# Band attention and two gated layers on one core: another order of the first loads

## The chip, the cores and the metric

The kernel runs on one core of one Trainium2 chip, as one program. The metric is the device time of one execution in microseconds (us): the median of several runs. A core has five engines with instruction streams of their own: TensorE (PE in the profile, its weight loads PEld), VectorE (DVE), ScalarE (ACT), GpSimd (POOL) and SyncE (SP, which here only issues loads). They meet through semaphores. Loads issued by SP go, in the order of issue, through one queue that all 16 DMA engines of the core serve.

## The reference, cut to what matters

There are 2 batches, 8 heads, 768 positions and 64 values for each head. Attention looks at a band of 16 positions to either side, and at one summary of each block of 32 positions: the maximum of the keys and the mean of the values.

```
k_sum = k.reshape(B, H, nb, block, D).max(axis=3)
v_sum = v.reshape(B, H, nb, block, D).mean(axis=3)
scores = [banded q @ k.T * scale ,  q @ k_sum.T * scale + log(block)]
x = softmax(scores) @ [v ; v_sum]                    # 1536 tokens x 512
x = (sigmoid(x @ w_gate) * (x @ w_val)) @ w_out      # 512 -> 1536 -> 512
y = max(x @ w1, x @ w2, x @ w3) @ w_out2             # 512 -> 768 -> 512
```

## The kernel before

**Units.** Attention is cut into 16 units (b, p, a): a batch, a pair of heads, a half of the 768 positions. Units 0 to 3 are batch 0, first half, pairs 0 to 3; units 4 to 7 its second half; units 8 to 15 are batch 1. A unit needs its keys (`kn`: all keys of a pair, for batch 1 also `kw`, windows laid out for it), its queries (`q`) and its value windows (`v`); a pair needs its values once more as whole rows (`vn`), for the block means. PE multiplies keys and queries (`scores`; the part `ks` against block maxima that DVE takes from `kn`), DVE takes maxima (L597), ACT exponentials (L603), DVE or ACT divides, PE transposes (L622), ACT copies (`at`), PE multiplies with the values (`pv`, L632), and ACT and DVE write the result as a high and a low part into a tile `x`. For batch 0 the block means come from PE: `vsum`, eight matmuls of `vn` with the constant `avg` (L520); for batch 1 POOL adds up rows first (L525).

**Weights.** A load `raw` brings 128x1024 words; DVE packs it in three operations (L405, L410, L414) into `c`; ACT (L348) and DVE (L351) split it into a high and a low part `w`. There are three buffers `raw`, two `c`, twelve `w`.

**Layers.** A projection of layer 1 (L711) is twelve matmuls of 128x384, into one of four PSUM banks `m`; it needs `x` of all four pairs of a half. Eight projections of a half (four gates, four values) make four tiles `h`; then `B` (L745) multiplies these with the weights of the output. First half, then second half, then the next group of four.

**Who sets the order.** Nothing is scheduled by hand and nothing while the program runs: `Plan.order` simulates the engines when the kernel is built, with a duration and a due time for each task, and writes the tasks down in that order. Each engine then works strictly in it. Constants such as `KEYS0` or `WLOAD0` say by how much a load is due ahead of its unit or weight. Where PE would wait for a tile in the first 45 us of the plan, the plan lets it run matmuls on zeros (`idle`, L994), whose result is overwritten.

Of the kernel before, what the change touches and what calls it, by code (L numbers as in the profile page):

```python
# [9 lines left out]
F32 = mybir.dt.float32  # L10
# [8 lines left out]
WIN = 16  # L19
# [8 lines left out]
LAST = 2  # L28
LASTACC = 12
KEYS0, KEYS = 14.0, 24.0  # L30
SUMS0, SUMS = 14.0, 8.0
ROWS0, ROWS = 2.0, 4.0
WLOAD = 24.0
WLOAD0 = 2.0
WREADY = 8.0
FREE_M = 2
BY_ACT = 6
# [3 lines left out]
SLACK = {"PE": 0.05, "DVE": 0.12, "ACT": 0.1, "POOL": 0.0, "SP": 0.0}  # L41
OVER = 0.0
BANKS_H, BANKS_W, BANKS_T = 7, 12, 5
BANKS_KW, BANKS_KN, BANKS_Q, BANKS_V = 2, 4, 3, 3


class Buf:
# [25 lines left out]
class Plan:  # L73
# [3 lines left out]
    LAT = {"PE": 0.0, "DVE": 0.13, "ACT": 0.05, "POOL": 0.1}  # L77
    CROSS = 0.17
    DMA = 0.95
    TABLE = 1.3  # L80

    def __init__(self):
# [2 lines left out]
    def add(self, eng, dur, due, fn, deps=(), new=(), uses=(), after=(), tab=None):  # L85
        t = Task(eng, dur, due, fn, [d for d in deps if d], list(new), list(uses), [d for d in after if d], tab)
        self.tasks.append(t)
        return t
# [26 lines left out]
    def order(self):  # L115
        engs = ("PE", "DVE", "ACT", "POOL", "SP")
        free = dict.fromkeys(engs, 0.0)
        free["SP"] = 0.6
        dge = ring = 0.0
        clock = self.Clock()  # L120
        free["PE"] = 1.13
        tab = "E"
        taken = {}
        wait, then, ready = {}, {}, {e: [] for e in engs}
        for t in self.tasks:
            pre = t.deps + t.after
            wait[t] = len(pre)
            for d in pre:
                then.setdefault(d, []).append(t)
            if not pre:  # L130
                ready[t.eng].append(t)
        out = []

        def earliest(t):
            at = free[t.eng]
            for d in t.deps:
                at = max(at, d.end + self.lag(d, t))
            for d in t.after:
                at = max(at, d.start)
            need = {}  # L140
            for b in t.new:
                k = need.get(b.tag, 0)
                need[b.tag] = k + 1
                used = taken.setdefault(b.tag, [])
                i = len(used) + k - b.n
                if i >= 0:
                    for d in used[i].users:
                        if d.end is None:
                            return None
                        at = max(at, d.end + (0.1 if d.eng != t.eng else 0.0))  # L150
            return at

        def pressing(x):
            return x[1].due + (SWITCH if x[1].tab and x[1].tab != tab else 0.0)

        while len(out) < len(self.tasks):
            best = None
            for e in engs:
                c = [(at, t) for at, t in ((earliest(t), t) for t in ready[e]) if at is not None]
                if not c:  # L160
                    continue
                first = min(at for at, _ in c)
                at, t = min((x for x in c if x[0] <= first + SLACK[e]), key=pressing)
                if best is None or at < best[0]:
                    best = at, t
            at, t = best
            ready[t.eng].remove(t)
            t.start = at
            t.end = at + t.dur
            if t.eng == "PE":  # L170
                if t.new and at < 45.0:
                    width = min(384, t.new[0].shape[-1] * (t.new[0].shape[1] if len(t.new[0].shape) == 3 else 1))
                    now = free["PE"]
                    while True:
                        end = clock.run(now, width / 2400.0, 1.0, False)
                        if end > at + OVER:
                            break
                        now = clock.run(now, width / 2400.0, 1.0) + 0.001
                        t.idle += 1
                    at = t.start = max(at, now)  # L180
                t.end = clock.run(at, t.dur, t.rows)
            if t.dma:
                dge = max(dge, at) + t.dma
                ring = max(ring, dge + 0.65) + (t.dur if t.eng == "SP" else 0.2)
                free[t.eng] = at + t.dur if t.eng != "SP" else dge + 0.025
                t.end = ring
            if t.tab and t.tab != tab:
                tab = t.tab
                t.end += self.TABLE
            if not t.dma:  # L190
                free[t.eng] = t.end
            for b in t.new:
                taken[b.tag].append(b)
            out.append(t)
            for d in then.get(t, ()):
                wait[d] -= 1
                if not wait[d]:
                    ready[d.eng].append(d)
        return out
# [3 lines left out]
def kernel(  # L203
# [15 lines left out]
    nc = tc.nc  # L219
    B, NPAIR, _, S = qt.shape  # L220
    D = vw.shape[-1]
# [6 lines left out]
    GF = 4  # L228
    NG = NF1 // GF
    TPU = HALF // 128  # L230
# [156 lines left out]
    def convert():  # L387
# [3 lines left out]
        def to_float(ck, t):  # L391
# [23 lines left out]
                    out=c.t, in0=half(r, 0), scalar=29, in1=c.t, op0=ALU.logical_shift_right, op1=ALU.bitwise_or)  # L415

            n += 1
            l = add("SP", 1.456, t - WLOAD - WLOAD0 * (n <= 10), load, new=[r], after=[prev.get("l")])
            k1 = add("DVE", 0.335, t - 2.7, c1, [l], [c], [r], [prev.get("1")])
            k2 = add("DVE", 0.602, t - 2.3, c2, [k1], [], [c, r])  # L420
            k3 = add("DVE", 0.602, t - 1.6, c3, [k2], [], [c, r])
# [69 lines left out]
        chain[tag] = t  # L491
        return t

    def load_task(tag, n, shape, src, dur, t):
        b = Buf(ap_, shape, F32, tag, n)

        def fn(what=tag):
            nc.sync.dma_start(out=b.t[0:src.shape[0]], in_=src)

        return b, after(tag, add("SP", dur, t, fn, new=[b]))  # L500

    kblock, vblock, pvs = {}, {}, {}
    attention = []

    def make_sums(b, p, T):

        kt, lk = load_task("kn", BANKS_KN, [128, S + 2 * WIN], kn[b, p], 1.14, T - (KEYS if b else KEYS0))
        r, lr = load_task("vn", 2, [96, 2, 8 * D], vn[b, p], 1.092, T - (SUMS if b else SUMS0))
        ks = Buf(ap_, [128, NB], F32, "ks", 4)
        vs = Buf(ap_, [128, 2 * D], F32, "vs", 4)  # L510
        ps = psum_s([128, 2 * D])
# [24 lines left out]
        if b == 0:  # L536
            v1, v2 = None, add("PE", 1.75, T - 5, vsum, [lr, built], [ps], [r])
        else:
            lr.after.append(pvs[4 + p])
            vr = Buf(ap_, [96, 2, D], F32, "vr", 2)  # L540
            v1 = add("POOL", 2.5, T - 8, vadd, [lr, built], [vr], [r])
            v2 = add("PE", 0.22, T - 5, vmean, [v1], [ps], [vr])
# [5 lines left out]
    def make_unit(u, i):  # L548
# [3 lines left out]
            make_sums(b, p, T)  # L552
        whole = b == 0
        ks, kk, kt, lk = kblock[b, p]
        if not whole:
            kt, lk = load_task("kw", BANKS_KW, [128, TPU, 2, CW], kw[b, p, a], 1.024, T - KEYS)
        q, lq = load_task("q", BANKS_Q, [128, HALF], qt[b, p, :, HALF * a:HALF * a + HALF], 0.546,
                          T - (KEYS0 if whole else KEYS))
        vt, lv = load_task("v", BANKS_V, [CW, TPU, 2, 2, D], vw[b, p, a], 0.82, T - (ROWS0 if whole else ROWS))
        vs, kv = vblock[b, p]  # L560
        e = [Buf(ap_, [128, TPU, CW], F32, f"e{h}", 2) for h in range(2)]
        nm = Buf(ap_, [128, 2, TPU], F32, "nm", 2)
# [392 lines left out]
        add("ACT", 0.52, due[key] + 4.5, store, [l], [o], [ps])  # L955

    built = add("POOL", 5.0, -100.0, build_consts)
    for i, u in enumerate(units):
        make_unit(u, i)
    convert()  # L960
# [94 lines left out]
```

## Time and profile before

| | us |
|---|---|
| median of 3 runs (564.14, 566.11, 566.13) | 566.11 |
| the profiled execution | 564.06 |
| its span, first to last instruction | 562.3 |
| PE busy | 543.9 (97% of the span) |
| DVE busy | 430.7 (77%) |
| ACT busy | 286.8 (51%) |
| POOL busy | 16.1 (3%) |

The shares are means over stretches with different limits: PE waits mostly in the first 80 us. A matmul's end is modelled, so a busy PE can hide short waits.

### The profile page before, as it was taken

What the parts mean: (1) busy time and instruction counts of PE and PEld (TensorE: products, weight loads), DVE (VectorE), ACT (ScalarE), POOL (GpSimd) and SP (SyncE); (2) the same over time, 40 slices, a digit from 0 to 9 for tenths busy, and PEclk for the clock granted to TensorE, in tenths of its full rate; (3) what the DMA queues carried; (4) which work ended last, traced back from release to release, by engine and by line L of the source; (5) the groups of instructions that cost most, each with busy time, mean ns of one, the idle gap of its engine ahead of it and who ended that gap; (6) DMA issues with size and microseconds to landing.
All of it is one profiled execution on the core that took longest, in us unless ns stands there. A gap on an engine that the chain in (4) does not pass through costs nothing.

```text
span 562.3 us, 10192 instructions
## 1 busy us (share of the span) xinstructions
PE 543.9 (97%) x3924; PEld 521.4 (93%) x3924; DVE 430.7 (77%) x987; ACT 286.8 (51%) x663; POOL 16.1 (3%) x30
## 2 busy tenths in 40 slices
PE   8689899999999999999999999999999999999997
PEld 7578799999999999999999999999999999997886
DVE  6789958894697598949996996799999997885000
ACT  4689776583765656966441332435344333453111
POOL 2001221100000000000000000000000000000000
PEclk9999999999999999999999999999999999999999
DMA  8999653563266453520652553120322222000111
GB/s 296 318 268 283 201 174 135 166 208 113 81 195 187 141 150 110 170 75 1 188 186 78 155 182 114 53 98 21 108 87 87 77 74 82 32 1 37 57 72 60
DMA packets 24288, 71.96 MB, mean 128 GB/s; under 512 B 2736, under 2 KB 6192, under 8 KB 24240
## 3 DMA queue, kind: packets, MB, share of 16 engines
q1 hardware_dynamic: 21120, 67.58, 38.7%
q10 hardware_dynamic: 3120, 3.74, 1.9%
q8 instruction: 31, 0.51, 0.4%
q14 instruction: 17, 0.14, 0.1%
HBM read 67.57 MB, written 3.15 MB: 126 GB/s over the span
## 4 chain that ended last, share of the span: by engine, by line
PE 81%; DVE 7%; DMA 5%; ACT 5%; issue 1%; SPq 1%; ACTq 0%; DVEq 0%
PE m L711 30%; PE m L745 16%; PE s L835 11%; PE m L835 11%; PE m L942 9%; DMA vn<-in_vn_dram 3%; PE s L632 2%; DMA raw<-in_wts_dram 1%; DVE c L414 1%; DVE c L410 1%; PE s L622 1%; ACT e L617 1%; ACT e L603 1%; DVE c L405 1%; PE s L590 1%
## 5 line engine op out<-in xcount | busy, mean ns | idle before, releaser
L711 PE MATMUL m<-x,w 128*128 128x384 f32 x1152 | 211.0, 338 | 0.5 <-ACT t L725 0.3
L711 PEld LDWEIGHTS m<-x,w 128*128 128x128 f32 x1152 | 198.7, 188 | 2.5 <-issue 0.6
L745 PE MATMUL m<-h,w 128*128 128x384 f32 x576 | 107.3, 338 | 0.7 <-DVE h L351 0.7
L745 PEld LDWEIGHTS m<-h,w 128*128 128x128 f32 x576 | 99.3, 188 | 2.0 <-DVE h L351 1.4
L348 ACT ACTIVATE w<-c 128x512 fp32r<-128x512 f32 x96 | 58.1, 610 | 71.6 <-DVE c L414 48.4
L351 DVE TENSOR_TENSOR w<-c,w 128x512 fp32r<-128x512 f32 x96 | 63.8, 665 | 12.6 <-ACT w L348 12.4
L414 DVE SCALAR_TENSOR_TENSOR c<-raw,c 128x512 int32<-128x512 int32 x96 | 66.7, 697 | 0.6
L410 DVE SCALAR_TENSOR_TENSOR c<-raw,c 128x512 int32<-128x512 int32 x96 | 66.0, 689 | 0.6
L835 PE MATMUL m<-x,w 128*128 128x384 f32 x294 | 56.3, 335 | 1.2 <-ACT t L850 1.2
L835 PE MATMUL s<-f,w 128*128 128x384 f32 x294 | 56.0, 334 | 0.0
L835 PEld LDWEIGHTS m<-x,w 128*128 128x128 f32 x294 | 51.3, 188 | 1.6 <-ACT t L850 1.5
L835 PEld LDWEIGHTS s<-f,w 128*128 128x128 f32 x294 | 51.4, 188 | 0.0
L405 DVE TENSOR_SCALAR c<-raw 128x512 int32<-128x512 int32 x96 | 41.7, 437 | 5.7 <-DMA raw<-in_wts_dram 4.7
L725 ACT ACTIVATE t<-m 128x384 f32<-128x384 f32 x48 | 23.4, 491 | 35.2 <-PE m L711 34.8
L730 DVE TENSOR_TENSOR t<-m,t 128x384 f32<-128x384 f32 x48 | 26.6, 554 | 15.3 <-PE m L711 10.8
L348 ACT ACTIVATE h<-t 128x384 fp32r<-128x384 f32 x48 | 24.9, 521 | 25.7 <-DVE t L730 23.8
L603 ACT ACTIVATE e<-e,nm 128x120 f32<-128x120 f32 x96 | 36.6, 384 | 1.3 <-DVE nm L597 1.1
L351 DVE TENSOR_TENSOR h<-t,h 128x384 fp32r<-128x384 f32 x48 | 26.9, 563 | 5.4 <-ACT h L348 5.4
L952 ACT ACTIVATE c<-m 128x512 f32<-128x512 f32 (+1 forms) x13 | 7.3, 565 | 40.0 <-PE m L942 39.6
L850 ACT ACTIVATE t<-s 128x384 f32<-128x384 f32 x27 | 13.3, 491 | 24.4 <-PE s L835 24.4
L942 PE MATMUL m<-w,x 128*128 128x512 f32 (+1 forms) x126 | 24.9, 359 | 0.0
L942 PE MATMUL m<-w,f 128*128 128x512 f32 x108 | 24.7, 389 | 0.0
(108 smaller groups left out, 586.4 us busy)
## 6 DMA issues: line engine op xcount, KB each, us to landing
raw<-in_wts_dram SPq DMA_DIRECT2D x96, 512.0 KB, 4.3
v<-in_vw_dram SPq DMA_DIRECT2D x16, 288.0 KB, 4.8
kn<-in_kn_dram SPq DMA_DIRECT2D x8, 400.0 KB
vn<-in_vn_dram SPq DMA_DIRECT2D x8, 384.0 KB
q<-in_qt_dram SPq DMA_DIRECT2D x16, 192.0 KB, 5.2
kw<-in_kw_dram SPq DMA_DIRECT2D x8, 360.0 KB, 10.0
out_dram<-c ACTq DMA_DIRECT2D x11, 256.0 KB, 2.0
v<-vs ACTq DMA_DIRECT2D x8, 72.0 KB
```

The source lines that it names most:

```text
L348: nc.scalar.activation(out=dst, in_=src, func=ACTF.Copy)
L351: nc.vector.tensor_tensor(out=dst, in0=src, in1=h.bitcast(F32), op=ALU.subtract)
L405: nc.vector.tensor_scalar(out=c.t, in0=half(r, 1), scalar1=5, scalar2=2, op0=ALU.logical_shift_left, op1=ALU.logical_shift_right)
L410: nc.vector.scalar_tensor_tensor(out=c.t, in0=half(r, 1), scalar=-0x40000000, in1=c.t, op0=ALU.bitwise_and, op1=ALU.bitwise_or)
L414: nc.vector.scalar_tensor_tensor(out=c.t, in0=half(r, 0), scalar=29, in1=c.t, op0=ALU.logical_shift_right, op1=ALU.bitwise_or)
L603: nc.scalar.activation(out=e[h].t[:, t], in_=e[h].t[:, t], func=ACTF.Exp, scale=-1.0, bias=nm.t[:, h, t:t + 1], accum_out=sm.t[:, h, t:t + 1])
L711: nc.tensor.matmul(ps.t, lhsT=w.t.rearrange("p s (k f) -> p s k f", k=KC)[:, wh, kc], rhs=src[kc // 2].t[:, xh, kc % 2], start=(kc == 0 an ...
L725: k1 = after("t", add("ACT", 0.371, end, lambda: nc.scalar.activation(out=s.t, in_=ps.t, func=ACTF.Sigmoid), [l], [s], [ps], tab="S"))
L730: k2 = after("t", add("DVE", 0.469, end, lambda: nc.vector.tensor_tensor(out=t.t, in0=ps2.t, in1=s.t, op=ALU.mult), [l2, k1], [t], [ps2, s]))
L745: nc.tensor.matmul(ps.t, lhsT=w.t.rearrange("p s (k f) -> p s k f", k=KC)[:, wh, dm], rhs=h.t[:, xh], start=(i == 0 and j == 0), stop=(i = ...
L835: nc.tensor.matmul(ps.t, lhsT=w.t[:, wh, c:c + 128], rhs=x.t[:, xh, kc], start=new and n == 0, stop=n == 5, skip_group_check=True)
L942: nc.tensor.matmul(ps.t[:, c0:c1], lhsT=h.t[:, xh, e, c:c + 128], rhs=w.t[:, wh, c0:c1], start=(f == 0 and i == 0), stop=(f == NF2 - 1 and ...
```

## The change

**Rows for the means.** The `vn` of batch 0 no longer have two buffers of their own: their loads go into the ring of eight tiles `x`, and take its first four places (they are issued as `x<-in_vn_dram`). Batch 1 keeps one buffer `vn`.

**First weights.** The first four weight loads are due one us behind the keys of units 0 to 3, not as early as possible; the rest of the first twelve by `WLOAD0`, now 12.

**Batch 1 held back.** The loads of unit i of batch 1 may stand in the order only behind the start of `pv` of unit i - 4, and `kn` and `vn` of a pair behind `pv` of unit 4 + p; before, only `vn` was held.

**The plan.** Due times of `vn` and `v` of batch 0 move (`SUMS0`, `ROWS0`), `v` has four buffers, and the plan takes transfers for 1.2 times as long. Since the plan decides the order, all engines' orders change. On PE the idle matmuls, 48 of 128 columns, 27 of 128 and 3 of 384 before, become 11 of 360, all ahead of the first scores.

```
-SUMS0, SUMS = 14.0, 8.0
-ROWS0, ROWS = 2.0, 4.0
+SUMS0, SUMS = 12.0, 8.0
+ROWS0, ROWS = 10.0, 4.0
-WLOAD0 = 2.0
+WLOAD0 = 12.0
-BANKS_KW, BANKS_KN, BANKS_Q, BANKS_V = 2, 4, 3, 3
+BANKS_KW, BANKS_KN, BANKS_Q, BANKS_V = 2, 4, 3, 4
...
+    SLOW = 1.2
...
-                ring = max(ring, dge + 0.65) + (t.dur if t.eng == "SP" else 0.2)
+                ring = max(ring, dge + 0.65) + (t.dur * self.SLOW if t.eng == "SP" else 0.2)
...
-            l = add("SP", 1.456, t - WLOAD - WLOAD0 * (n <= 10), load, new=[r], after=[prev.get("l")])
+            at = target[units[n - 1]] - KEYS0 + 1.0 if n <= NPAIR else t - WLOAD0 if n <= 3 * GF else t - WLOAD
+            l = add("SP", 1.456, at, load, new=[r], after=[prev.get("l")])
...
+    def make_rows(p):
+        r = Buf(xp, [96, 2, 8 * D], F32, "x", 8)
+        vrows[p] = r, after("x", add(
+            "SP", 1.092, target[0, p, 0] - SUMS0, lambda: nc.sync.dma_start(out=r.t, in_=vn[0, p]), new=[r]))
...
-        kt, lk = load_task("kn", BANKS_KN, [128, S + 2 * WIN], kn[b, p], 1.14, T - (KEYS if b else KEYS0))
-        r, lr = load_task("vn", 2, [96, 2, 8 * D], vn[b, p], 1.092, T - (SUMS if b else SUMS0))
+        kt, lk = load_task("kn", BANKS_KN, [128, S + 2 * WIN], kn[b, p], 1.14, T - (KEYS if b else KEYS0), [pvs[NPAIR + p]] if b else [])
+        if b == 0:
+            r, lr = vrows[p]
+        else:
+            r, lr = load_task("vn", 1, [96, 2, 8 * D], vn[b, p], 1.092, T - SUMS, [pvs[NPAIR + p]])
...
+        held = [] if whole else [pvs[i - NPAIR]]
         if not whole:
-            kt, lk = load_task("kw", BANKS_KW, [128, TPU, 2, CW], kw[b, p, a], 1.024, T - KEYS)
+            kt, lk = load_task("kw", BANKS_KW, [128, TPU, 2, CW], kw[b, p, a], 1.024, T - KEYS, held)
...
+    for p in range(NPAIR):
+        make_rows(p)
```

On SP, at the very start of the program, the first twelve loads before (the numbers tell tiles apart; `raw` is a weight, the rest belongs to batch 0):

```order
L398 DMA raw_119<-in_wts_dram 128x1024
L498 DMA kn_121<-in_kn_dram 128x800
L498 DMA vn_123<-in_vn_dram 96x1024
L498 DMA q_125<-in_qt_dram 128x384
L398 DMA raw_127<-in_wts_dram 128x1024
L398 DMA raw_129<-in_wts_dram 128x1024
L498 DMA kn_131<-in_kn_dram 128x800
L498 DMA vn_133<-in_vn_dram 96x1024
L498 DMA q_137<-in_qt_dram 128x384
L498 DMA v_140<-in_vw_dram 96x768
L498 DMA kn_144<-in_kn_dram 128x800
L498 DMA q_146<-in_qt_dram 128x384
```

and with the change:

```order
L501 DMA kn_119<-in_kn_dram 128x800
L501 DMA q_121<-in_qt_dram 128x384
L399 DMA raw_123<-in_wts_dram 128x1024
L514 DMA x_125<-in_vn_dram 96x1024
L501 DMA v_127<-in_vw_dram 96x768
L501 DMA kn_129<-in_kn_dram 128x800
L501 DMA q_131<-in_qt_dram 128x384
L399 DMA raw_133<-in_wts_dram 128x1024
L514 DMA x_137<-in_vn_dram 96x1024
L501 DMA v_168<-in_vw_dram 96x768
L501 DMA kn_170<-in_kn_dram 128x800
L501 DMA q_172<-in_qt_dram 128x384
```

Keys and queries of unit 0 now stand first, one weight goes between the loads of two units, and `vn` and `v` follow their unit.

On SP, the two loads `kw` of batch 1 stood before among the keys, weights and values of batch 0 (these are the 14th to 19th load):

```order
L498 DMA kn_208<-in_kn_dram 128x800
L398 DMA raw_212<-in_wts_dram 128x1024
L498 DMA v_215<-in_vw_dram 96x768
L498 DMA kw_217<-in_kw_dram 128x720
L498 DMA vn_241<-in_vn_dram 96x1024
L498 DMA kw_245<-in_kw_dram 128x720
```

and now the first `kw` is the 37th, behind eleven weights (the 33rd to 40th load):

```order
L399 DMA raw_696<-in_wts_dram 128x1024
L399 DMA raw_729<-in_wts_dram 128x1024
L399 DMA raw_781<-in_wts_dram 128x1024
L501 DMA kn_801<-in_kn_dram 128x800
L501 DMA kw_807<-in_kw_dram 128x720
L501 DMA q_817<-in_qt_dram 128x384
L501 DMA vn_820<-in_vn_dram 96x1024
L501 DMA v_844<-in_vw_dram 96x768
```

What moved: both `kw` left the stretch in which batch 0 is loaded, and all loads of the first unit of batch 1 stand together.

On DVE, the rows up to the low part of the third tile `h` of the first half, `h_1100` before:

```order
L730 TENSOR_TENSOR t_1058<-m_996,t_1035 128x384
L514 TENSOR_REDUCE ks_1080<-kn_686 128x24
L405 TENSOR_SCALAR c_1082<-raw_921 128x512
L572 COPY kw_217<-ks_1080 128x3x24 x2
L410 SCALAR_TENSOR_TENSOR c_1082<-raw_921,c_1082 128x512
L351 TENSOR_TENSOR h_1100<-t_1033,h_1100 128x384
```

and the same tile, here `h_1003`, with the change:

```order
L411 SCALAR_TENSOR_TENSOR c_966<-raw_864,c_966 128x512
L528 TENSOR_REDUCE ks_1005<-kn_801 128x24
L415 SCALAR_TENSOR_TENSOR c_966<-raw_864,c_966 128x512
L352 TENSOR_TENSOR h_1003<-t_962,h_1003 128x384
L623 TENSOR_SCALAR sm_827<-sm_827 128x6
L624 RECIPROCAL sm_827<-sm_827 128x6
L352 TENSOR_TENSOR x_842<-s_947,x_842 128x384
L352 TENSOR_TENSOR w_1031<-c_966,w_1031 128x512
```

What moved: the packing of the 13th weight (`c_1082`) and the copy into `kw` stood ahead of it before and stand behind it now, as do one product `t` and the low part of the twelfth weight (`w_1031`, before `w_1012`, further up).

## Rows read from the trace of the kernel before

**Rows 1.** Busy time by stretch: window, length, PE, PEld, DVE, ACT, POOL, clock, DMA share, GB/s.
```profile
0.00:10.00 10.00, 8.17 (x112) 7.81 (x112) 4.79 (x9) 2.69 (x4) 3.92 (x18) 1.00 0.82 285
10.00:25.00 15.00, 9.94 (x192) 8.47 (x187) 13.01 (x59) 10.26 (x38) 0.00 (x0) 1.00 1.04 337
25.00:40.00 15.00, 13.09 (x208) 11.41 (x208) 12.11 (x45) 11.61 (x37) 0.00 (x0) 1.00 1.04 256
40.00:60.00 20.00, 17.41 (x217) 15.58 (x217) 19.89 (x53) 17.55 (x45) 3.25 (x3) 1.00 0.80 254
60.00:80.00 20.00, 19.43 (x206) 17.44 (x208) 15.96 (x52) 15.55 (x52) 4.97 (x5) 1.00 0.73 226
...
200.00:500.00 300.00, 299.72 (x1846) 297.48 (x1845) 261.39 (x524) 138.71 (x283) 0.00 (x0) 1.00 0.32 99
```
**Rows 2.** Timeline of PE, 0 to 70 us: start, length, instruction, idle time before it.
```profile
1.19 5.30 PE L994 MATMUL s<-idle 128*128 128x128 bf16 x48 [1.19 <-DVE idle L984]
...
7.14 2.02 PE L520 MATMUL s<-vn,avg 96*128 96x128 f32 x16 [0.64 <-DMA vn<-in_vn_dram]
...
10.06 1.68 PE L994 MATMUL s<-idle 128*128 128x128 bf16 x27
...
12.55 2.05 PE L520 MATMUL s<-vn,avg 96*128 96x128 f32 x16 [0.81 <-DMA vn<-in_vn_dram]
...
22.07 0.51 PE L622 MATMUL m<-ident,e 128*120 128x128 f32 x3 [1.85 <-DVE sm L608]
...
24.83 2.05 PE L520 MATMUL s<-vn,avg 96*128 96x128 f32 x16 [1.07 <-DMA vn<-in_vn_dram]
...
26.82 0.92 PE L632 MATMUL s<-at,v 120*64 120x64 f32 x24
...
60.12 0.51 PE L622 MATMUL s<-ident,e 128*120 128x128 f32 x3 [1.78 <-DVE e L612]
...
62.06 1.21 PE L745 MATMUL m<-h,w 128*128 128x384 f32 x6
...
66.94 2.21 PE L745 MATMUL m<-h,w 128*128 128x384 f32 x11 [0.43 <-DVE h L351]
```
**Rows 3.** Timeline of DVE: the rows that waited for a landing.
```profile
4.44 0.43 DVE L405 TENSOR_SCALAR c<-raw 128x512 int32<-128x512 int32 x1 [3.31 <-DMA raw<-in_wts_dram]
...
16.89 0.95 DVE L514 TENSOR_REDUCE ks<-kn 128x24 f32<-128x768 f32 x1 [1.25 <-DMA kn<-in_kn_dram]
...
19.66 0.95 DVE L514 TENSOR_REDUCE ks<-kn 128x24 f32<-128x768 f32 x1 [0.60 <-DMA kn<-in_kn_dram]
...
34.19 0.43 DVE L405 TENSOR_SCALAR c<-raw 128x512 int32<-128x512 int32 x1 [0.51 <-DMA raw<-in_wts_dram]
...
38.28 0.43 DVE L405 TENSOR_SCALAR c<-raw 128x512 int32<-128x512 int32 x1 [0.85 <-DMA raw<-in_wts_dram]
```
**Rows 4.** Timeline of POOL: its first adding of rows.
```profile
54.04 2.54 POOL L525 TENSOR_TENSOR vn<-vn 96x512 f32<-96x512 f32 x2 [48.96 <-PE s L622]
```
**Rows 5.** Timeline of DVE in and just behind that stretch.
```profile
54.58 1.41 DVE L405 TENSOR_SCALAR c<-raw 128x512 int32<-128x512 int32 x1
...
57.92 0.41 DVE L405 TENSOR_SCALAR c<-raw 128x512 int32<-128x512 int32 x1
...
58.86 0.68 DVE L410 SCALAR_TENSOR_TENSOR c<-raw,c 128x512 int32<-128x512 int32 x1
```
**Rows 6.** Groups of ACT, 44.4 to 82.6 us: busy and mean, idle before.
```profile
L603 ACT ACTIVATE e<-e,nm 128x120 f32<-128x120 f32 x18 | 6.9, 384 | 0.0
...
L725 ACT ACT_TABLE_LOAD x3 | 3.8, 1283 | 0.0
...
L617 ACT ACTIVATE e<-e,sm 128x120 f32<-128x120 f32 x12 | 3.7, 382 | 2.4 <-DVE sm L609 2.4
...
L348 ACT ACTIVATE w<-c 128x512 fp32r<-128x512 f32 x5 | 3.0, 624 | 2.9 <-DVE c L414 2.9
...
L348 ACT ACTIVATE x<-s 128x384 fp32r<-128x384 f32 x4 | 1.9, 475 | 1.7 <-PE s L632 1.7
```

More of the change, by code (lines that the diff above doesn't have):

```diff
@@ L492, in after, with load_task @@
         return t
-    def load_task(tag, n, shape, src, dur, t):
+    def load_task(tag, n, shape, src, dur, t, held=()):
         b = Buf(ap_, shape, F32, tag, n)
@@ L498, in fn @@
             nc.sync.dma_start(out=b.t[0:src.shape[0]], in_=src)
-        return b, after(tag, add("SP", dur, t, fn, new=[b]))
+        return b, after(tag, add("SP", dur, t, fn, new=[b], after=held))
     kblock, vblock, pvs = {}, {}, {}
     attention = []
-    def make_sums(b, p, T):
-        kt, lk = load_task("kn", BANKS_KN, [128, S + 2 * WIN], kn[b, p], 1.14, T - (KEYS if b else KEYS0))
-        r, lr = load_task("vn", 2, [96, 2, 8 * D], vn[b, p], 1.092, T - (SUMS if b else SUMS0))
+    vrows = {}
+    def make_rows(p):
+        r = Buf(xp, [96, 2, 8 * D], F32, "x", 8)
+        vrows[p] = r, after("x", add(
+            "SP", 1.092, target[0, p, 0] - SUMS0, lambda: nc.sync.dma_start(out=r.t, in_=vn[0, p]), new=[r]))
+    def make_sums(b, p, T):
+        kt, lk = load_task("kn", BANKS_KN, [128, S + 2 * WIN], kn[b, p], 1.14, T - (KEYS if b else KEYS0), [pvs[NPAIR + p]] if b else [])
[3 more added lines that the diff above has]
+            r, lr = load_task("vn", 1, [96, 2, 8 * D], vn[b, p], 1.092, T - SUMS, [pvs[NPAIR + p]])
         ks = Buf(ap_, [128, NB], F32, "ks", 4)
@@ L538, in make_sums @@
         else:
-            lr.after.append(pvs[4 + p])
             vr = Buf(ap_, [96, 2, D], F32, "vr", 2)
@@ L554, in make_unit @@
         ks, kk, kt, lk = kblock[b, p]
+        held = [] if whole else [pvs[i - NPAIR]]
         if not whole:
-            kt, lk = load_task("kw", BANKS_KW, [128, TPU, 2, CW], kw[b, p, a], 1.024, T - KEYS)
+            kt, lk = load_task("kw", BANKS_KW, [128, TPU, 2, CW], kw[b, p, a], 1.024, T - KEYS, held)
         q, lq = load_task("q", BANKS_Q, [128, HALF], qt[b, p, :, HALF * a:HALF * a + HALF], 0.546,
-                          T - (KEYS0 if whole else KEYS))
-        vt, lv = load_task("v", BANKS_V, [CW, TPU, 2, 2, D], vw[b, p, a], 0.82, T - (ROWS0 if whole else ROWS))
+                          T - (KEYS0 if whole else KEYS), held)
+        vt, lv = load_task("v", BANKS_V, [CW, TPU, 2, 2, D], vw[b, p, a], 0.82, T - (ROWS0 if whole else ROWS), held)
         vs, kv = vblock[b, p]
```

## Prediction

> **What bounds it now.** I read first where PE is not at work, by stretch. From 200 to 500 us it is busy 299.7 of 300 us, and up to 80 us it loses 12.0: 1.8, 5.1 and 1.9 in the first 40 us (windows of 10, 15 and 15), 2.6 in the next 20, 0.6 in the last 20 [rows 1]. To these come the matmuls on zeros, which count as busy: 48 from 1.19 us and 27 at 10.06 [rows 2]. What the change can win, it wins there; the work behind is the same.
>
> The timeline of PE says what it waited for [rows 2]: nothing real until 7.14 us, where the first `vn` lands; 2.5 us of zeros and waiting up to the second at 12.55; 1.85 for DVE at 22.07; 1.1 for the third `vn` at 24.83, which stands in front of the second `pv` (26.82); 1.8 for DVE at 60.12. The first `B` begins at 62.06, and at 66.94 it has waited for the third `h`.
>
> Two things stand behind these waits. From 10 to 40 us the DMA engines are never idle (share 1.04), at 337 GB/s first and at 256 from 25 us on. From 40 to 60 us DVE is busy 19.89 of 20 us, after 10.1 idle in the first 40 (40 less 4.79, 13.01 and 12.11) [rows 1]. So transfers bound the first 40 us and DVE the next 25. POOL makes DVE's stretch longer: it adds rows from 54.04 [rows 4], and a packing operation of DVE that takes 0.41 us just behind it takes 1.41 in it [rows 5].
>
> **When a load lands now.** Summing the loads in SP's order gives the KB up to each (raw 512, kn 400, vn 384, kw 360, v 288, q 192, from their shapes); where an engine waited for a landing, the trace gives the time. 512 KB: 4.4 us; 1296: 7.1; 3296: 12.5; 4176: 16.9; 5056: 19.7; 6600: 24.8; 9040: 34.2; 10032: 38.3 [rows 2, 3]. In between I go linearly, and read the new order on the same curve, since both bring the same mixture of tiles through one queue:
>
> First scores (592 KB) 4.7 us. First weight (1104) 6.4 against 4.4 before. First `vn` (1488) 7.6 against 7.1, but it no longer stands ahead of the first scores, which had to wait for it and its `vsum` of 2.02 [rows 2]. Second `q` (2368) 10.0. Third `vn` (5040) 19.6 against 24.8. Fourth `q` (7104) 26.8, before (7664) 28.9. Fourth `v` (6912) 26.0 against 32.2 (8528). Fifth weight (7616) 28.7, before (7472) 28.2; seventh (9600) 36.5 against 38.3. So attention gets its data 2 to 6 us earlier, two `kw` (720 KB) less ahead of it, and the weights, which bound DVE, hardly earlier.
>
> **Step by step.** *Order of the first loads.* DVE has the same operations, so I count its idle time. Before: 10.1 us. With the change: until the first `kn` lands 3.9 (400 KB instead of 512, so a few tenths before 4.4); 1.4 from the end of its maxima at about 5.0 to the first weight at 6.4; 0.7 for ACT's copy of it, which DVE waits for in either order; 1.2 for the fifth weight at 28.7, since DVE has done all that stands ahead of it by 27.5; 0.4 for the seventh; 0.3 in small waits. Together 7.9, and a gain of **2.2**. Bounds: if the transfers ran from 25 us on at 337 GB/s as before that, the two waits for weights are gone (3.8); if the first landings come 1 us later than on the curve, 1.2. I take the curve's own value, because raws, `v` and `q` alternate from there in both orders.
>
> [...]
>
> *PE follows.* It stays ahead of DVE. The clearest place is the second `pv`: the third `vn` is there at 19.6, its `vsum` of 2.05 has to come in between, and `pv` can begin at about 22.3 instead of 26.82 [rows 2]. Fewer zeros cost nothing here, because PE still waits for the transfers they covered.
>
> *Order on DVE.* Up to the low part of the third `h` 2.3 us less stands ahead: two operations of the thirteenth weight, the low part of the twelfth, one product and the copy into `kw` (0.4 for the first packing operation, 0.6 for the second and for a low part, as a row of 0.68 starts its successor some 0.1 early; 0.4 for the product and 0.3 for the copy by their smaller size) [rows 5]. In the DVE-bound stretch this is **2.3** for whoever waits for that `h`: PE at 66.94, with 0.43 of wait [rows 2], would go on at about 62.4. PE can be there: its first `B` comes at 57 to 59. So 4.5 at this point. POOL's adding, with the `vn` of batch 1 landing at about 50, still falls into this stretch, as before.
>
> *Held loads, batch 1.* The order puts units 8 and 9 earlier on all engines: their scores now stand among the `B` of the first half, before behind 51 projections of the second. Taking from 44.4 us to the first gate of the second half, ACT idles 7.0 us now (2.4, 2.9 and 1.7, for the softmax and packing of DVE and for `pv` [rows 6]) in 38.2. The change puts into the same part of its order four more exponentials of a head (three of 0.384 each), two more divisions of a head (three of 0.382), two more table loads (1.28), in all 9.5 [rows 6], some of it overlapped: about 9. It begins some 3 us earlier and has 7 of idle time to fill, but an idle engine is not always idle at the right moment. PE has four banks `m`; if ACT comes late to the first gate of the second half, PE stops after 48 projections. Nothing (0) if the idle time takes it all, 3 if a third of the 9 does not fit. I take **1.0** of loss, nearer to none since the idle time is almost as long as the added work.
>
> *Waiting on SP.* The third `kw` waits for the scores of unit 8 (two buffers), and weights queue up behind it; but the weights from the 13th on wait for one of twelve `w` anyway, until the second half uses the first. Nothing. *Sizes of rings* (`v` four instead of three, `vn` one): nothing; POOL is nearly idle there (3.25 of 20 us [rows 1]).
>
> *Clock.* [...] I take **0.5** for a rise some microseconds later; below, what it costs if it is much later.
>
> **Sum.** 2.2 + 2.3 - 1.0 - 0.5 = **3.0 us**. Against the profiled execution's 564.06 that is 561.1 (span 562.3 to 559.3). That execution is the fastest of those shown; with the median of 566.11 the forecast is **563.1**. 0.5% of it, 2.8 us, is about what a measurement of this kernel tells from no change: the forecast lies on that edge.
>
> **The rivals.** *A, more (20%).* The stretch from 25 us runs at 337 GB/s, the idle time of ACT takes all of unit 8 and 9, the clock rises as early as now: 3.8 + 2.3 = 6.1, so 560.0. For it: no row ties the lower rate to what is loaded. Against: it lasted 15 us, over the same kinds of tiles that stand there now.
>
> *B, the clock stays low, nothing is won (23%).* [...] The same result would come, if the landings lag behind the sum of KB by more than now, so that the order does not do what it says.
>
> *C, slower (12%).* ACT is late. From its first gate at about 41 us to the first gate of the second half it has 31 + 9 = 40 us of work; PE needs it at about 84. With 7 us of waiting as now it would be 88, PE stops for 4, and with the clock's 0.5 all is given back; POOL's second and third adding in the same stretch, each up to 2 us on DVE as at 54 [rows 4, 5], push it to 91. Then 4.5 is won and 7 lost: 568.6. It decides from those 7 us of waiting on ACT between these two points. Against: the plan knows ACT's durations, and put other work of PE ahead of each transpose there.
>
> **How the numbers follow.** The forecast's own case (45%) spans 561 to 564.5; its better part is beyond 0.5%. Faster by over 0.5%: A and 28 of the 45, **0.48**. Within: the other 17 and B, **0.40**. Slower: C, **0.12**. The range from 559.8 to 567.2 leaves out the outer half of C and an edge of A.
>
> **What would show it.** First scores at about 5 us; third `vsum` at 20 to 21; second `pv` near 22; DVE's idle time to 40 us near 8; `B` at 57 to 59; third `h` let go near 62.4; no wait of PE over 1 us from 70 to 90. Wrong it is, if the `vsum` start with spacings of the low level beyond 15 us, if DVE waits for the weights as long as now, or if ACT is late for the first gate of the second half.

## The result, and the profile after

| | before | with the change |
|---|---|---|
| median of the runs (us) | 566.11 (564.14 to 567.61, 9 runs) | 570.76 (567.19 to 572.33, 9 runs) |
| ratio | | 1.0079, 95% interval 1.0056 to 1.0102 |
| profiled execution / its span (us) | 564.06 / 562.3 | 570.35 / 568.6 |

The change makes the kernel slower by 0.8%. The forecast was 563.1 with a range up to 567.2: wrong in sign, and outside.

Windows of the changed kernel, columns as in [rows 1]:

```profile
0.00:10.00 10.00, 4.51 (x59) 2.49 (x59) 2.26 (x4) 1.28 (x1) 3.68 (x18) 0.91 0.77 201
10.00:25.00 15.00, 12.93 (x163) 11.87 (x164) 11.74 (x48) 9.62 (x34) 0.00 (x0) 0.60 1.04 256
25.00:40.00 15.00, 11.96 (x185) 10.63 (x185) 10.69 (x42) 10.60 (x32) 0.00 (x0) 0.89 1.05 240
40.00:60.00 20.00, 18.15 (x247) 16.09 (x240) 19.46 (x64) 19.15 (x53) 0.00 (x0) 1.00 0.78 241
60.00:80.00 20.00, 16.44 (x169) 13.90 (x167) 19.90 (x67) 16.41 (x50) 7.00 (x6) 1.00 0.82 249
...
200.00:500.00 300.00, 299.72 (x1864) 297.17 (x1863) 259.63 (x521) 140.53 (x285) 0.00 (x0) 1.00 0.31 98
```

From 10 to 40 us the DMA engines are as busy as before (share 1.04 and 1.05) but move 256 and 240 GB/s, where [rows 1] have 337 and 256. DVE's idle time up to 40 us is 40 less 2.26, 11.74 and 10.69, so 15.3 us: before 10.1, forecast 7.9. The work behind is the same (200 to 500 us).

The timeline of DVE, its rows that wait for a landing, answers to [rows 3]:

```profile
3.88 0.95 DVE L528 TENSOR_REDUCE ks<-kn 128x24 f32<-128x768 f32 x1 [2.74 <-DMA kn<-in_kn_dram]
...
8.88 0.43 DVE L406 TENSOR_SCALAR c<-raw 128x512 int32<-128x512 int32 x1 [4.04 <-DMA raw<-in_wts_dram]
...
16.24 0.43 DVE L406 TENSOR_SCALAR c<-raw 128x512 int32<-128x512 int32 x1 [1.16 <-DMA raw<-in_wts_dram]
...
32.15 0.43 DVE L406 TENSOR_SCALAR c<-raw 128x512 int32<-128x512 int32 x1 [0.59 <-DMA raw<-in_wts_dram]
...
36.86 0.43 DVE L406 TENSOR_SCALAR c<-raw 128x512 int32<-128x512 int32 x1 [2.36 <-DMA raw<-in_wts_dram]
```

These are the first keys and the first, second, fourth and fifth weight. The keys are there as early as forecast. The first weight (1104 KB) comes at 8.88, by the curve at 6.4; the second (2880) at 16.24, by the curve at 11.4; the fourth (6624) at 32.15, by the curve at 24.9; the fifth (7616) at 36.86, forecast 28.7.

The timeline of PE answers to [rows 2]:

```profile
1.20 3.48 PE L1011 MATMUL s<-idle 128*128 128x360 bf16 x11 [1.20 <-DVE idle L1001]
...
10.95 3.76 PE L534 MATMUL s<-x,avg 96*128 96x128 f32 x16 [5.24 <-DMA x<-in_vn_dram]
...
25.43 2.02 PE L534 MATMUL s<-x,avg 96*128 96x128 f32 x16
...
27.38 0.92 PE L647 MATMUL s<-at,v 120*64 120x64 f32 x24
...
30.38 2.19 PE L534 MATMUL s<-x,avg 96*128 96x128 f32 x16 [2.08 <-DVE e L627]
...
65.72 1.31 PE L760 MATMUL m<-h,w 128*128 128x384 f32 x6
...
69.54 1.67 PE L760 MATMUL m<-h,w 128*128 128x384 f32 x8 [0.64 <-DVE h L352]
...
75.44 1.84 PE L760 MATMUL m<-h,w 128*128 128x384 f32 x9 [1.33 <-ACT t L740]
```

The first sum of rows waits 5.24 us for its load and then takes 3.76 us instead of 2.02, at the lower clock (0.60 from 10 to 25 us in the windows). The third sum is at 25.43, the second `pv` at 27.38, the first `B` at 65.72 and the `h` that was to be let go at 62.4 at 69.54. At 75.44 PE waits 1.33 for ACT's first gate of the second half.

What stands out are the first microseconds behind the small loads. One window, 4 to 6 us, of the kernel before and of the changed one:

```profile
4.00:6.00 2.00, 2.00 (x22) 2.00 (x20) 1.40 (x3) 0.00 (x0) 0.90 (x4) 1.00 1.03 375
```

```profile
4.00:6.00 2.00, 1.71 (x51) 1.02 (x49) 0.83 (x1) 0.00 (x0) 0.66 (x4) 1.00 0.70 209
```

The first weight of the changed kernel was issued at 1.71 us and the next four loads by 3.6; still, from 4 to 6 us, the engines are busy for 0.70 of the time, and 209 GB/s pass instead of 375.

### The profile page after: what moved, and what is told of

Read it like the earlier page. It is cut to its first block, busy times and chain, and to the rows that moved or that the text cites. A ratio compares the mean times of both kernels' runs of the same rounds, so it can differ in the third digit from the quotient of the medians.

```text
span 568.6 us, 10054 instructions
## 1 busy us (share of the span) xinstructions
PE 546.0 (96%) x3857; PEld 522.0 (92%) x3857; DVE 431.0 (76%) x987; ACT 285.0 (50%) x661; POOL 15.9 (3%) x30
## 3 DMA queue, kind: packets, MB, share of 16 engines
HBM read 67.57 MB, written 3.15 MB: 124 GB/s over the span
## 4 chain that ended last, share of the span: by engine, by line
PE 78%; DVE 9%; DMA 6%; ACT 5%; issue 1%; SPq 1%; ACTq 0%; DVEq 0%
PE m L726 28%; PE m L760 16%; PE s L850 11%; PE m L850 11%; PE m L957 9%; DMA raw<-in_wts_dram 6%; DVE c L411 2%; DVE c L415 1%; DVE w L352 1%; PE s L647 1%; ACT L740 1%; DVE e L612 1%; DVE c L406 1%; ACT e L618 1%; PE s L637 1%; ACT e L632 1%
## 5 line engine op out<-in xcount | busy, mean ns | idle before, releaser
L957 PE MATMUL m<-w,x 128*128 128x512 f32 (+1 forms) x126 | 24.9, 359 | 0.0
```

Of the source, the lines that this page charges most:

```text
L957: nc.tensor.matmul(ps.t[:, c0:c1], lhsT=h.t[:, xh, e, c:c + 128], rhs=w.t[:, wh, c0:c1], start=(f == 0 and i == 0), stop=(f == NF2 - 1 and ...
```

## The experiments

The first theory: the loads run slower in the new order, and everything else follows. Rivals: the loads are slow because of what the engines do beside them; or PE's lower clock costs the time.

**Loads alone.** A kernel with nothing but the first loads, each into a tile of its own; all computation is left out. `ORDER` lists the loads in the order of the kernel in question:

```diff
...
+        for what in ORDER:
...
+            nc.sync.dma_start(out=t, in_=src)
...
+        for j, (what, t) in enumerate(zip(ORDER, tiles)):
+            nc.vector.tensor_copy((seen if what == "raw" else tiny)[0:t.shape[0], j:j + 1], t[:, 0:1])
```

> Only the first 31 loads of the kernel before, in its order, each into a tile of its own, with one column of each read by DVE in order; all computation is left out and zeros are stored. If the order of the loads sets the rate (theory T), they run at 350 to 400 GB/s for the first 20 us, as in the kernel before, and the weight that ends 5568 KB is there by about 20 us. If the rate is set by what the engines do beside the transfers (rival W), this run and the next one have the same rate, within 10%.

> Only the first 31 loads of the changed kernel, in its order, each into a tile of its own; all computation is left out. Theory T: the rate drops to about 235 GB/s when the first load of 96 partitions is followed by another one (from about 4 us), and 5040 KB take 20 us or more. Rival W: 350 to 400 GB/s as in the other order, 5040 KB by about 15 us.

> The loads of the changed kernel in its order, but the rows for the means and the values are laid over 128 partitions instead of 96, with the same bytes; all computation is left out. If the alternation of loads of 96 and of 128 partitions makes the transfers slow, they now run at 350 to 400 GB/s throughout, 5040 KB by about 15 us. If the order as such does it (which part of the memory is read when), the rate stays at about 235 GB/s.

In these three 3.15 MB of stores of zeros ran beside the loads, so that the start tells nothing. From 25 to 40 us both orders moved about the same (326 and 330 GB/s, share 1.04); the third had 354 at a share of 0.92, since its loads ended in that window. They were repeated with the stores behind the last load:

> As the first kernel with loads alone (order of before, first 32 loads, all computation left out), but the stores wait for the last load, so that only loads move. If the loads of 96 partitions disturb the transfers wherever they stand (theory S, shape), the rate swings between 230 and 410 GB/s from the first of them on, as it did after 21 us in the first such run (mean 326 from 25 to 40 us). If it is the order (theory O), it stays near 400 for the first 20 us.

> The loads of the changed kernel in its order, alone, all computation left out, the stores behind the last load. Theory O: about 235 GB/s from 4 us on, the 15th load (5328 KB) no earlier than 20 us. Theory S: the same swings as in the other order, means within 10% of each other, the 15th load at about 17 us.

> The same order with the rows for the means and the values over 128 partitions, the same bytes, stores last, all computation left out. Theories S and O for the shape: about 405 GB/s throughout, as after 21 us in the first such run, the 15th load by about 15.5 us. If only the stores had made the difference there, it swings like the other two.

Windows from 10 to 25 us (DVE, POOL, clock, share, GB/s), in this order:

```profile
10.00:25.00 15.00, 2.12 (x14) 0.00 (x0) 1.00 1.04 329
```

```profile
10.00:25.00 15.00, 1.67 (x11) 0.00 (x0) 1.00 1.04 278
```

```profile
10.00:25.00 15.00, 2.62 (x17) 0.00 (x0) 1.00 1.04 409
```

With the same share of 1.04 the engines move 329, 278 and 409 GB/s, so engines that count as busy all the time move very different amounts. The last load was read at 36.96, 43.10 and 32.36 us (11.49 MB in the order of before, 11.04 in the other two). So no engine's work is needed to make the new order slow: that rival falls for the most part. Both theories of the loads were half right: loads over 96 partitions among loads over 128 slow the transfers in either order, and the new order is slower still. The same bytes over 128 partitions run at 409.

Two windows go against taking the rate for a property of the order alone. The first is the new order from 25 to 40 us with the stores at its start, the second the same order without them:

```profile
25.00:40.00 15.00, 2.13 (x14) 0.00 (x0) 1.00 1.04 330
```

```profile
25.00:40.00 15.00, 1.83 (x12) 0.00 (x0) 1.00 1.04 279
```

The last load was read at 43.07 and at 43.10 us, though 3.15 MB of stores went through as well in the first. So the same loads in the same order ran at different rates (one execution each), by what had gone before. And the order of before shows alone no drop behind 25 us, where the whole kernel falls from 337 to 256 [rows 1]:

```profile
25.00:36.00 11.00, 1.68 (x11) 0.00 (x0) 1.00 1.04 325
```

What takes the rate down there in the whole kernel, no run shows.

Why loads over 96 partitions move less than the same bytes over 128 (278 against 409 GB/s), no run here shows.

**Clock.** The changed kernel with more matmuls on zeros:

```diff
+        nsum = 0
...
+            if t.fn.__name__ == "vsum":
+                t.idle += {0: 85, 3: 35}.get(nsum, 0)
+                nsum += 1
```

> The changed kernel with 85 more matmuls on zeros ahead of the first sum of rows and 35 ahead of the fourth, so that PE has no long gap up to 32 us. Theory T (late transfers cost the time): the clock stays at its high level, but the time falls by less than 1.5 us from 570.8, since PE and DVE wait for the loads anyway. Rival C (the lower clock costs the time): 3 us or more come back, 566 to 568.

```profile
0.00:10.00 10.00, 8.80 (x133) 6.85 (x133) 2.54 (x5) 1.28 (x1) 3.68 (x18) 1.00 0.80 212
10.00:25.00 15.00, 10.99 (x179) 9.71 (x176) 12.16 (x48) 10.19 (x35) 0.00 (x0) 0.89 1.04 256
25.00:40.00 15.00, 13.15 (x228) 11.95 (x229) 10.76 (x43) 10.79 (x36) 0.00 (x0) 0.98 1.04 260
```

The clock is up (0.89 instead of 0.60 from 10 to 25 us), the loads are as slow as before (256 GB/s), and the time is 571.11 us (568.13 to 573.11), ratio 1.0107 (1.0048 to 1.0167). The rival of the clock (C in that expectation, not the prediction's C) falls, as long as the loads are late: with the two intervals taken together the clock could have given back some 2 us at most, not 4.5.

**128 rows in the whole kernel.** The 32 rows that follow in memory come along unused:

```diff
-        r = Buf(xp, [96, 2, 8 * D], F32, "x", 8)
+        r = Buf(xp, [128, 2, 8 * D], F32, "x", 8)
+        rows = vn.rearrange("b p r h d -> (b p r) h d")[96 * p:96 * p + 128]
...
+        vsrc = vw[b, p, a] if i >= 12 else vw.rearrange("b p a r t q h d -> (b p a r) t q h d")[at0:at0 + 128]
```

> The changed kernel with the same order of all instructions; the rows for the means of batch 0 and all values but the last four units' are loaded as 128 rows instead of 96 (the 32 rows that follow in memory come along and are not used, a third more bytes for them). If loads of 96 partitions are what slows the transfers in the whole kernel too, the rate from 6 to 40 us rises from 235 to 380 GB/s or more, DVE idles less than 12 us up to 40 us instead of 15.3, and the time falls by 3 to 6 us, to 565 to 568. If it is what the engines do beside the transfers, the rate stays at about 240 GB/s, and the added 1.3 MB make it slower by 2 us or more.

```profile
10.00:25.00 15.00, 11.82 (x179) 10.68 (x178) 13.69 (x59) 8.92 (x33) 0.00 (x0) 1.00 1.04 404
25.00:40.00 15.00, 8.87 (x104) 8.38 (x106) 5.77 (x14) 8.62 (x24) 0.00 (x0) 0.66 0.40 136
```

```profile
29.72 0.84 ACT L599 ACTIVATE v<-vs 24x768 f32<-24x768 f32 x1 [8.21 <-DMA v<-in_vw_dram]
```

The rate is 404 GB/s at the same share, beside all the work of the engines: for the rate the theory holds. The time went the wrong way, 575.42 us, ratio 1.0180 (1.0150 to 1.0211). The row of ACT shows why: its copy into partitions 96 to 119 of a tile of values now has to wait for the load that writes there too, 8.21 us in one piece, and everything queued behind it on ACT waits as well. That is a fault of this experiment, not of the transfers. The next four take it apart:

> The changed kernel with ROWS0 back to 2: the values of the first units leave the place right behind the rows for the means and stand later; the rest of the change stays. If it is the neighbourhood of two loads of 96 partitions that makes the engines of the DMA fall out of step (theory N), the rate from 10 to 25 us rises from 256 towards 330 GB/s and some 2 to 4 us come back, 567 to 569. If any mixture of 96 and 128 partitions does it as badly (theory M), the rate stays at 250 to 270 GB/s and the time within 1.5 us of 570.8.

> The changed kernel with its order of instructions; only the four loads of rows for the means of batch 0 are 128 rows (32 unused rows more each), the values stay at 96. ACT's copies into the values wait for nothing more than before. Theory N: with no two loads of 96 partitions in a row the rate from 6 to 25 us rises to 320 GB/s or more, and 2 to 4 us come back, 567 to 569. Theory M: the values alone suffice, 260 to 290 GB/s and less than 1.5 us.

> The changed kernel with 128 rows for the means of batch 0 and for the values of the first twelve units, planned with ACT's copy into a tile of values behind its load, the longer loads, and transfers at the rate that the last such run showed (factor 0.9 instead of 1.2). If the slow transfers alone took what the forecast promised, the new order at 400 GB/s gives the forecast, DVE's idle time up to 40 us near 8 and 561 to 565 us. If the order costs time elsewhere too (ACT, units 8 and 9, the clock), it stays at 567 or more though the rate is at 400 GB/s.

> The kernel before, same order, with the four loads of rows for the means of batch 0 as 128 rows instead of 96 (512 KB more in all). If 96 partitions cost there as well, its rate from 10 to 25 us rises from 337 to 380 GB/s or more, which pays for the added bytes: 563 to 566 us. If the loads stay as they are, the added 0.5 MB cost up to 1.5 us.

```diff
# rows0_back
-ROWS0, ROWS = 10.0, 4.0
+ROWS0, ROWS = 2.0, 4.0
# pad2_fill_late, beside the 128 rows
-    SLOW = 1.2
+    SLOW = 0.9
-        g1 = add("ACT", 0.12 if dma else 0.83, T - 5, lambda: vfill(dma), [kv], [], [vt, vs], [lv])
+        g1 = add("ACT", 0.12 if dma else 0.83, T - 5, lambda: vfill(dma), [kv, lv] if i < 12 else [kv], [], [vt, vs], [lv])
```

| | median (us) | ratio to before | GB/s 10 to 25, 25 to 40 us |
|---|---|---|---|
| ROWS0 back to 2 | 568.27 | 1.0051 (1.0025 to 1.0076) | 258, 265 |
| only the sums' rows as 128 | 567.23 | 1.0032 (1.0009 to 1.0055) | 324, 237 |
| 128 rows, copies planned behind | 562.76 | 0.9950 (0.9933 to 0.9967) | 403, 241 |
| before, sums' rows as 128 | 563.94 | 0.9962 (0.9946 to 0.9977) | 345, 285 |

The rate rises where the sums' rows are widened (324 instead of 256), not where the values move (258): theories N and M each got one. Widening does two things at once, it parts two loads of 96 partitions that stood side by side and it leaves fewer such loads; which of the two counts is not told apart. Two versions beat both kernels. The third row of the table reaches the forecast's time with a rate of 403 GB/s up to 25 us, but it was planned anew, so its gain is not that of the rate alone. DVE's idle time up to 40 us is 9.7 us there, not the 8 expected, and so hardly less than the 10.1 of before:

```profile
10.00:25.00 15.00, 14.17 (x182) 12.92 (x183) 14.38 (x61) 11.79 (x43) 0.00 (x0) 0.69 1.03 403
25.00:40.00 15.00, 12.42 (x209) 10.64 (x210) 12.98 (x51) 13.05 (x44) 0.00 (x0) 0.89 0.65 241
40.00:60.00 20.00, 17.88 (x206) 16.25 (x207) 19.22 (x46) 15.31 (x35) 3.01 (x3) 1.00 0.69 240
60.00:80.00 20.00, 20.00 (x188) 19.00 (x187) 15.96 (x52) 18.08 (x54) 5.49 (x6) 0.91 0.87 285
80.00:120.00 40.00, 40.00 (x309) 38.43 (x308) 31.98 (x85) 30.42 (x74) 2.01 (x2) 1.00 0.52 166
```

**The first three loads.** Open was why one order is slower than the other, when both hold loads of 96 partitions. The changed kernel, all in the same order but for its first weight, which goes to the front of the queue:

```diff
+        tasks = plan.order()
+        loads = [t for t in tasks if t.eng == "SP"]
+        tasks.remove(loads[2])
+        tasks.insert(tasks.index(loads[0]), loads[2])
```

> The loads of the changed kernel alone (all computation left out, stores behind the last load), in its order but for one place: the first weight stands ahead of the first keys and queries. If the small first loads throw the engines of the DMA out of step (theory G), no gap shows at 4 to 6 us, 1104 KB are there at about 5.5 us instead of 8.1, and the mean rate from 10 to 25 us rises from 278 to 320 GB/s or more. If the neighbourhood of the loads of 96 partitions does it (theory N), the gap may go, but the rate from 10 to 25 us stays at 260 to 290 GB/s.

> The changed kernel with its first weight ahead of the first keys and queries, everything else in the same order. Theory G: the first weight is there at 4.5 us instead of 8.9, the first rows for the means by 6.5 instead of 10.9, the rate from 10 to 25 us is above 300 GB/s, and 3 us or more come back, 565 to 568. Theory N: the first weight is early, but the rate from 10 us on stays at about 250 GB/s, and 2 us or less come back, 568.5 to 570.

Alone, from 10 to 25 us, and in the whole kernel, from 4 to 6 us:

```profile
10.00:25.00 15.00, 1.84 (x13) 0.00 (x0) 1.00 1.03 303
```

```profile
4.00:6.00 2.00, 0.68 (x3) 0.02 (x1) 0.62 (x1) 0.00 (x0) 0.68 (x4) 1.00 1.03 297
```

Alone, the first 1104 KB were read by 5.94 us instead of 8.11, and the rate from 10 to 25 us rose from 278 to 303, between what the two theories said. In the whole kernel the window from 4 to 6 us is full (share 1.03, 297 GB/s), and the time is 566.11 us (10 runs, 564.33 to 568.48), ratio 1.0004 (0.9982 to 1.0026). One place in the queue gives back 4.2 of the 4.5 us (1.0079 less 1.0004, of 566; by the two intervals 2.4 to 6.0). The rate from 10 to 25 us is 285 GB/s there, again between the theories. The mirror of it, the kernel before with keys and queries ahead of its first weight and nothing else moved:

```diff
+        tasks = plan.order()
+        loads = [t for t in tasks if t.eng == "SP"]
+        for x in (loads[1], loads[3]):
+            tasks.remove(x)
+            tasks.insert(tasks.index(loads[0]), x)
```

> The kernel before with its first keys and queries ahead of its first weight on the queue of loads, nothing else moved. Theory G (small first loads leave a part of the DMA engines without work for 2 to 3 us, and their skew slows what follows): the first weight is there at about 8 us instead of 4.4, and the time rises by 2 to 4 us. By the sum of KB alone it would be there at 6.4 us, and since the first scores stand behind the first rows for the means anyway, the time would rise by at most 2 us.

```profile
8.86 0.43 DVE L405 TENSOR_SCALAR c<-raw 128x512 int32<-128x512 int32 x1 [7.73 <-DMA raw<-in_wts_dram]
```

```profile
74.20 2.21 PE L745 MATMUL m<-h,w 128*128 128x384 f32 x11 [0.43 <-DVE h L351]
```

```profile
10.00:25.00 15.00, 13.41 (x234) 11.95 (x234) 12.15 (x44) 9.61 (x33) 0.00 (x0) 0.82 1.05 261
```

These are a row of DVE, a row of PE and the window from 10 to 25 us. The first weight is there at 8.86 instead of 4.44, the wait for the third `h` ends at 74.20 instead of 66.94 [rows 2, 3], the rate is 261 GB/s instead of 337 [rows 1] with the same loads behind, and the time is 570.15 us, ratio 1.0093 (1.0071 to 1.0114): more than theory G allowed, and as much as the whole change costs. Two reservations. The executions that the profiles show took 568.48 and 572.37 us, each 2.2 to 2.4 us above the median, so these rows show rather much lateness, and the medians say what the edits are worth. And the clock moved with the loads (from 10 to 25 us 0.95 instead of 0.60 with the weight in front, 0.82 instead of 1.00 in the mirror), so a part of the 4.2 and of the 5.0 can be the clock's.

In eleven runs without stores beside the loads, the first microseconds went with the first three loads. With keys and queries in front, six moved 204 to 260 GB/s from 4 to 6 us, at shares from 0.63 to 0.99; with the weight in front, five moved 297 to 375, at 0.87 to 1.03. The first three loads do not decide the rate behind by themselves. Alone and with all loads over 128 partitions, this was the window from 4 to 6 us:

```profile
4.00:6.00 2.00, 0.15 (x1) 0.00 (x0) 1.00 0.63 204
```

The first weight was read as late as 7.95 us there, and yet 409 GB/s passed from 10 to 25 us. So a slow start was followed by 256 GB/s (the changed kernel), 261 (the mirror) and 278 (the loads alone) from 10 to 25 us, where rows for the means and values over 96 partitions came behind it, and by 409 where all loads had 128.

Three more runs tried to add up what helped; the weight is moved, and the sums' rows are widened, by the lines above:

```diff
# pad2_zeros
+            if t.fn.__name__ == "vsum":
+                t.idle += {0: 55}.get(nsum, 0)
```

> The version with loads of 128 rows and ACT's copies behind them, with 55 more matmuls on zeros ahead of the first sum of rows. With the transfers fast, PE's lower clock from 9 to 19 us (first sum of rows 3.75 us instead of 2.0) can cost: if it does, 1 to 2 us come back, 561 to 562; if DVE waits for weights and ACT all the same, it stays within 0.7 us of 562.8.

> The version with loads of 128 rows and ACT's copies behind them, with the first weight ahead of the first keys and queries. If the gap at 4 to 6 us costs DVE the time that it waits for the first weight there (2.9 us), some 2 us come back, 560.5 to 561.5; if only the clock or ACT limits it by then, 562 to 563.

> The changed kernel with the first weight in front and the four loads of rows for the means as 128 rows, all else in the same order. If both faults of the loads add up, 2 us or more below the run with the weight in front alone: 562 to 564.5 us, ratio to before 0.995 to 0.998. If the values of 96 partitions keep the rate low or ACT and the clock limit by then, 565 to 567 us.

They gave 563.52 (0.9963, 0.9948 to 0.9977), 562.66 (0.9952, 0.9935 to 0.9968) and 565.57 us (1.0008, 0.9992 to 1.0024). None gained on the version that it started from. In the second the weight in front, worth 4.2 us in the changed kernel, was worth nothing in this version, whose loads have 128 rows and whose plan is another: what an early first weight is worth hangs on what follows it. The first settles nothing about the clock, which stayed at 0.66 from 10 to 25 us in spite of the zeros. The last is told below.

## Why the prediction was wrong

**What bounds it** was right: transfers up to 40 us, then DVE.

**The step that failed is the landing curve**, "read the new order on the same curve, since both bring the same mixture of tiles through one queue". The rate was taken as a property of the mixture; with the same mixture it hangs on the order and on how the queue started. With small loads in front (592 KB of keys and queries) the window from 4 to 6 us moves 209 GB/s instead of 375, and the first weight, which DVE needs next, comes 2.5 us behind the curve. What follows stays slow (256 GB/s instead of 337 from 10 to 25 us), and the fifth weight is 8.2 us late. The forecast's 2.2 us of gain on DVE's idle time up to 40 us became a loss of 5.2 (15.3 against 10.1). Shown both ways: weight in front, 4.2 us back; keys in front in the kernel before, 5.0 lost, with the rate down to 261. The weight in front brings the rate from 256 only to 285, so the rest of the order has its part too. That the rate hangs on the shape is shown as well (278 against 409 GB/s for the same bytes). Rival A's "no row ties the lower rate to what is loaded" had a point: what lowered the rate of the kernel before from 25 us on was not its loads alone (325 GB/s without computation).

**Order on DVE, 2.3.** Right, and a little more. Windows of DVE up to the point where the third `h` lets PE go, in the kernel before, in the changed one, and in the version with the weight in front and 128 rows for the sums:

```profile
0.00:66.94 66.94, 56.73 (x187) 1.00 0.91 278
```

```profile
0.00:69.54 69.54, 53.66 (x181) 0.88 0.93 251
```

```profile
0.00:64.87 64.87, 53.55 (x181) 0.95 0.90 277
```

The change takes six operations and 3.1 us of work out of DVE's way to this `h` (56.73 less 53.66). About 1 us of that stood beside POOL's adding: before, a first packing operation took 1.41 us while POOL added [rows 4, 5], which the prediction took to stay; with the change all twelve first packing operations up to here take 0.42 to 0.49. What is lost is idle time: 10.2 us before (66.94 less 56.73), 15.9 with the change (69.54 less 53.66). So 5.7 more idle and 3.1 less work make the 2.6 us by which `h` is late.

In the version with the weight in front and 128 rows for the sums, DVE's idle time up to 40 us is 9.4 (40 less 4.17, 13.67 and 12.80), 0.7 less than before. Up to `h` it has idled 11.3 us (64.87 less 53.55), 1.1 more than before. Timeline of PE there:

```profile
64.87 1.68 PE L761 MATMUL m<-h,w 128*128 128x384 f32 x8 [0.63 <-DVE h L352]
...
70.77 7.30 PE L761 MATMUL m<-h,w 128*128 128x384 f32 x30 [1.33 <-ACT t L741]
```

The wait for `h` ends at 64.87, 2.1 us earlier than 66.94 [rows 2]: 3.2 less work, 1.1 more idle time. The forecast had 4.5 at this point.

**Held loads, 1.0.** Too small. Groups of PE with their idle time, first in the changed kernel from 66 to 92 us, then in the version that was planned anew from 60 to 92:

```profile
L760 PE MATMUL m<-h,w 128*128 128x384 f32 x48 | 10.0, 349 | 3.2 <-DVE h L352 1.4 <-ACT t L740 1.3 <-DVE t L745 0.5
...
L605 PE MATMUL s<-kw,q 64*64 64x120 f32 x48 | 2.4, 274 | 1.3 <-ACT at L640 1.1 <-DVE kw L587 0.2
```

```profile
L763 PE MATMUL m<-h,w 128*128 128x384 f32 x48 | 10.2, 351 | 0.0
...
L608 PE MATMUL s<-kw,q 64*64 64x120 f32 x48 | 1.7, 271 | 0.0
```

In the order of the change PE waits 1.3 us for ACT's first gate of the second half, and 1.1 for tiles that ACT copies behind a transpose: 2.4 in place of 1.0. (With the weight in front, from 60 to 92 us, it is 1.3 and 1.1 as well.) So rival C's mechanism is there, at a third of its price of 7. It takes the 2.1 that this version won at `h`, which fits its ending at 1.0008 and not at the forecast. For the profiled executions the account closes. `h` is let go 2.6 us later than before (69.54 against 66.94). The 25 us behind it, in the kernel before and in the changed one:

```profile
66.94:91.94 25.00, 24.98 (x199) 23.16 (x200) 16.81 (x48) 15.92 (x45) 4.97 (x5) 1.00 0.43 130
```

```profile
69.54:94.54 25.00, 21.14 (x194) 18.78 (x195) 15.20 (x65) 21.01 (x73) 6.13 (x6) 1.00 0.68 201
```

PE is idle for 0.02 us there before and for 3.86 now; with the 2.6 that makes 6.4, for the 6.3 us measured (570.35 less 564.06). In the version planned anew these waits are gone (PE busy 60 of 60 us from 60 to 120). That the new plan is the cause of its last 2 to 3 us fits this, but it was not undone by itself.

**Clock, 0.5**, and rival B. No run shows the term of 0.5. What they show in its place: the clock stayed low as B had it (0.50 from 10.95 to 14.71 us, where the first sum of rows took 3.76; the second, at 18.78, took 3.42, and only the third, at 25.43, took 2.02, at 1.00), and raising it to 0.89 from 10 to 25 us gave nothing that the runs can tell while the loads were late (ratio 1.0107 against 1.0079). "Fewer zeros cost nothing here" holds so far as that run can tell. B's sentence that the landings may lag behind the sum of KB named the real cause, but at a price of nothing won instead of 5 us lost.

## What to carry to other kernels

A table of bytes against landing times holds for the order that it was read from; before loads are reordered, look at GB/s at full DMA share by stretch, and at which shapes stand there. Try a large load that someone needs at the front of the queue (4.2 us here, but nothing in the version with 128 rows that was planned anew), and try 128 rows in place of 96 where spare rows cost little (2.2 us in the kernel before, 0.0038 of 566); but then see who writes the other partitions of that tile. A late landing moved what stood behind it: in the mirrored run the first weight came 4.4 us later (8.86 against 4.44), the third `h` 7.3 us later (74.20 against 66.94), and the profiled execution took 8.3 us longer (572.37 against 564.06).

## What was not expected of the hardware

Where loads over 96 partitions stand among loads over 128, full DMA engines (share 1.03 to 1.05) moved anything from 256 to 345 GB/s from 10 to 25 us without stores beside them, by the order, the number of such loads and what had gone before; as 128 rows they moved 403 to 409. And behind two small first loads (400 and 192 KB) the engines were busy for only 0.70 of the time from 4 to 6 us (209 GB/s), with 512 KB in front for 1.03 (297). Why the engines stand still there stays open: the trace does not say what they wait for. In the mirrored run the share was 0.99 at 260 GB/s, so there the engines counted as busy and were slow.
